# Opening three quarters of the first tile's layer_in one pair of heads at a time

## The chip, the cores and the metric

The kernel runs on one NeuronCore of a Trainium2 chip. The time is the device time of one execution in microseconds (us), median of three. The core has five engines that follow their own instruction lists: PE (matmul and transpose), DVE (vector), ACT (activation), POOL, and SP, which issues the loads and stores.

## What is computed

A sparse attention, a first feed-forward layer with the activation h * cos(h), and a layer of eight experts of which each token uses one:

```
scores = (q @ k.T) / 8                      # 2 batches x 8 heads x 576 x 576
scores = where(scores >= 32nd largest of the row, scores, -1e9)
x = softmax(scores) @ v                     # -> 1152 tokens x 512
h = x @ w_in                                # 512 -> 2048
x = (h * cos(h)) @ w_out                    # 2048 -> 512
expert, gate = argmax, max of softmax(x @ w_gate)
out = gate * (relu(x @ w1[expert]) @ w2[expert])
```

The weights w_in and w_out arrive as 64-bit numbers; the kernel converts them to 32-bit ones itself.

## The kernel before

**Attention** runs in 36 steps. A step takes 128 queries of a pair of heads (a few steps are shaped otherwise). `scores` makes a 128 x 576 score matrix for each head of the pair in one PSUM tile S (two banks, one tile only), half at a time; a copy on ACT or DVE puts the first half into Sp. `pair_chain` folds the halves on DVE into C and finds the 32 largest of each row by MAX8 and MATCH_REPLACE8 (lines 852 to 859). `softmax` subtracts the penalty, takes exp on ACT (L900) and scales. `products` transposes the result in three groups of three (tile pt, two banks, L927), copies each to PT, and multiplies by v into av (L941, L943). An ACT copy (L980) stores av as one quarter, one pair of heads, of the tile's input xn.

**Tiles.** Four steps make up one tile of 128 tokens; tile 0 takes steps 0 to 3. `layer_in` (L1021 for the first two tiles) computes its 2048 hidden features in four units u of four blocks of 128: for each block it adds four matmuls, kc = 0 to 3, one for each quarter of xn, in one PSUM bank, h. So no matmul of unit u of tile 0 could start before step 3 had filled the last quarter. The unit is copied to hs and its bank is free for the next one; there is one h bank. Then follow a clamp, the cosine, the product, and `layer_out` (L1106), which adds 16 blocks in one of the two banks x2. A routing step, a scatter and a gather lead to the experts (L1472 to L1536).

**Weights.** `convert(n)` turns block n of the weights into 32 bits: a load, an ACT operation whose result `lo` is held in a PSUM bank (L698), a conversion wt on ACT or POOL, and one or two DVE operations of which one reads `lo` (L704, L712). For n below 16 it is w_in, n = 4u + kc. The bank of `lo` is taken from the two banks x2.

**Unread products.** `unread` (L1264) makes 24 groups of eight bf16 matmuls of a constant by itself in the early part. They are written to a bank of x2 and never read.

**The order.** Each operation has a number. ORDER lists all of them; a program goes through the list, gives each operation its buffers and appends it to its engine's instruction list, so an engine's order is fixed when the kernel is built, and an engine waits where the next instruction of its list waits. PICKS says for each operation that could run on two or three engines which one has it. A tile that shares a `tag` with another shares its buffers.

Of the kernel before, what the change touches and what calls it, by code (L numbers as in the profile page):

```python
# [8 lines left out]
F32 = mybir.dt.float32  # L9
F32R = mybir.dt.float32r  # L10
BF = mybir.dt.bfloat16
I32 = mybir.dt.int32
# [37 lines left out]
    "0000020000000000000000210000000020000000020001000200010000110000000200000000000010000010000000010000"  # L50
    "0000000000000210101000000100000000000001000000000000000010000000000000000001100001000000010000000010"
    "0000000100022000000000000010002101000010000000001000000020000110010000000000100100010000000002111011"
    "0221110101220010111020010110111011111000110011101111111100000000100000000100111100100101011101110101"
    "0111011100001111110100111111110101000000000000000001110110110110010000100000010001000011011011010001"
    "0100000100000101011101110110000100010101001001111010000000000000000000100001110100010111010101011101"
    "011010101001")
ORDER = [
# [192 lines left out]
GROUPS = (0, 1, 2, 4, 6, 8, 9)  # L250
PLAIN = 2
UNCUT = 6
UNREAD = 24


class Nothing:
# [293 lines left out]
def forward(ctx, lasting, tc, kq, vn, vs_, w_in, w_out, w_gate, w1, w2, out, paired):  # L550
# [448 lines left out]
    def transposes(kp, src):  # L999
        for c in range(4):  # L1000
            PE.transpose(T[kp][:, c * 128:(c + 1) * 128], src()[:, c * 128:(c + 1) * 128], ident)

    def layer_in(t, u):


# [662 lines left out]
```

## Time and profile before

| | us |
|---|---|
| runs (three) | 632.49, 634.88, 634.97 |
| median | 634.88 |
| profiled execution | 633.3 |
| its span, first to last instruction | 631.5 |

The span is cut into stretches below. "Busy" is the time in which an engine has an instruction running. PE's matmuls overlap in the records, so the time from one start to the next is the better cost of one. The column PEclk is the granted clock of PE as a share of 2.4 GHz; where no change of it is on record it reads 1.00, and then the matmuls' own durations tell the level.

### The profile page before, as it was taken

To read this page: it belongs to the slowest core of one execution; us is meant where nothing else is said; L and a number is where in the kernel's file an instruction comes from. 1 tells how busy PE (TensorE), PEld (TensorE's weight loads), DVE (VectorE), ACT (ScalarE), POOL (GpSimd) and SP (SyncE) were. 2 spreads that over 40 slices of the span, in tenths; PEclk is the share of its full clock that TensorE was granted. 3 is DMA by queue.
4 is the path that set the end of the run, shared out by engine and by line. 5 is a ranking of instruction groups with operands and counts; after the bars stand their busy time and mean duration, and the time that the engine had idled before them with its cause. 6 is when DMAs were issued, how large, how long until landed. Compare 5 with 4: busy or idle time off the path is not lost.

```text
span 631.5 us, 11976 instructions
## 1 busy us (share of the span) xinstructions
PE 581.7 (92%) x4000; PEld 457.4 (72%) x4000; DVE 523.9 (83%) x1503; ACT 482.5 (76%) x999; POOL 338.9 (54%) x441
## 2 busy tenths in 40 slices
PE   2486999999999999999999999999889999999994
PEld 0264685675568767777677887888679898888993
DVE  5999999999999999999999896475466788878772
ACT  4899899999988888989788767546536686876762
POOL 3678778898886887856667343135661021020111
PEclk9998799999999999999999999999979999999998
DMA  8857995522343322331212100343356778776740
GB/s 318 302 158 247 330 376 184 183 61 69 108 122 88 87 83 68 109 109 46 88 45 83 43 22 19 109 142 117 122 168 201 221 253 246 220 237 224 230 146 17
DMA packets 44614, 94.64 MB, mean 150 GB/s; under 512 B 7165, under 2 KB 11261, under 8 KB 44544
## 3 DMA queue, kind: packets, MB, share of 16 engines
q1 hardware_dynamic: 42800, 89.04, 44.4%
q0 software_dynamic: 1744, 4.76, 2.0%
q8 instruction: 33, 0.54, 0.4%
q14 instruction: 37, 0.30, 0.1%
HBM read 81.87 MB, written 12.69 MB: 150 GB/s over the span
## 4 chain that ended last, share of the span: by engine, by line
PE 50%; DVE 12%; ACT 7%; issue 6%; POOL 2%; POOLq 0%; DVEq 0%; ACTq 0%
PE yp L1517 8%; PE x L1106 6%; PE x L1114 5%; PE hp L1472 5%; PE av L941 3%; PE hp L1477 3%; PE h L1031 3%; PE pt L927 2%; PE h L1033 2%; PE h L1032 2%; PE S L812 2%; DVE C L855 2%; PE h L1026 2%; DVE W L852 2%; PE hp L1475 1%
## 5 line engine op out<-in xcount | busy, mean ns | idle before, releaser
L897 POOL TENSOR_TENSOR Sp<-Sp,pen 128x576 f32<-128x576 f32 x67 | 86.6, 1292 | 31.3 <-ACT pen L893 31.1
L855 DVE MATCH_REPLACE8 C<-W,C 128x288 f32<-128x288 f32 x216 | 94.8, 442 | 0.0
L852 DVE MAX8 W<-C 128x8 f32<-128x288 f32 x216 | 93.2, 450 | 1.5
L1522 POOL DMA_INDIRECT out_dram<-ot,ti x16 | 17.2, 1073 | 127.5 <-DVE ot L1536 92.7
L812 PE MATMUL S<-kq 64*128 64x288 f32 x256 | 52.9, 493 | 27.0 <-DVE C L840 11.7
L1106 PE MATMUL x<-wo,hs 128*128 128x512 f32 x148 | 75.2, 607 | 0.1
L893 ACT ACTIVATE pen<-Sp,tb 128x576 bf16<-128x576 f32 x72 | 55.6, 772 | 6.4 <-POOL Sp L897 3.7
L927 PEld LDWEIGHTS pt<-ident,Sp 128*128 128x128 f32 x324 | 38.1, 143 | 28.1 <-issue 10.1
L900 ACT ACTIVATE Sp<-Sp,tb 128x576 f32<-128x576 f32 x72 | 55.7, 774 | 3.3 <-POOL Sp L897 1.7
L927 PE MATMUL pt<-ident,Sp 128*128 128x128 f32 x324 | 52.5, 282 | 4.5 <-ACT lo L698 2.1
L812 PEld LDWEIGHTS S<-kq 64*128 64x128 f32 x256 | 21.1, 200 | 47.1 <-issue 22.9
L1033 PE MATMUL h<-xh,wl 128*128 128x256 f32 x192 | 54.1, 282 | 0.0
L859 DVE MAX8 W<-C 128x8 f32<-128x576 f32 x72 | 52.9, 752 | 0.8
L670 ACT ACTIVATE PT<-pt 128x384 f32<-128x384 f32 x92 | 43.3, 486 | 10.4 <-PE pt L927 9.7
L840 DVE TENSOR_TENSOR C<-S,Sp 128x576 f32<-128x576 f32 x64 | 47.4, 749 | 3.3 <-ACT Sp L670 2.1
L670 ACT ACTIVATE Sp<-S 128x576 f32<-128x576 f32 x59 | 38.1, 646 | 9.9 <-PE S L812 7.2
L941 PEld LDWEIGHTS av<-PT,v 128*64 128x64 f32 x320 | 35.9, 142 | 13.1 <-issue 4.0
L941 PE MATMUL av<-PT,v 128*64 128x128 f32 x320 | 44.4, 287 | 0.9 <-DVE xl L974 0.8
L943 PE MATMUL av<-PT,v 128*64 128x128 f32 x320 | 44.2, 287 | 0.3 <-ACT PT L670 0.2
L1477 PE MATMUL hp<-xgs,la 128*128 128x192 f32 (+2 forms) x160 | 39.7, 251 | 0.0
L1472 PE MATMUL hp<-xgs,wk 128*128 128x384 f32 x128 | 38.9, 361 | 0.1
L1090 POOL TENSOR_TENSOR hs<-hs,ur 128x512 f32<-128x512 f32 x25 | 32.8, 1316 | 11.2 <-ACT ur L1081 11.1
(225 smaller groups left out, 1883.1 us busy)
## 6 DMA issues: line engine op xcount, KB each, us to landing
raw<-in_w_dram SPq DMA_DIRECT2D x64, 512.0 KB, 3.9
kq<-in_kq_dram SPq DMA_DIRECT2D x40, 288.0 KB, 2.9
v<-in_vn_dram SPq DMA_DIRECT2D x32, 320.0 KB, 3.5
wraw<-in_w_in_dram SPq DMA_DIRECT2D x16, 512.0 KB, 5.3
wraw<-in_w_out_dram SPq DMA_DIRECT2D x16, 512.0 KB, 4.2
xs<-z SPq DMA_DIRECT2D x1, 4680.0 KB, 19.0
v<-in_vs_dram SPq DMA_DIRECT2D x8, 320.0 KB, 3.3
out_dram<-z SPq DMA_DIRECT2D x1, 2304.0 KB, 24.2
```

The costliest lines, as they stand in the source:

```text
L670: P.flex([("act", act, lambda: ACT.activation(*args(), AF.Copy, scale=scale), False), ("dve", dve, lambda: DVE.tensor_scalar(*args(), scal ...
L812: PE.matmul(T[kp][:, a, 0:HS], t[p, S:S + 128], t[p, i * HS:(i + 1) * HS], start=True, stop=True)
L852: P.op("dve", 0.372, lambda r=r, i=i: DVE.max(T["W", s][:, i, LIST[r]:LIST[r] + 8], T["C", s][:, i, 0:HS]), r=[("C", s, i)], w=[("W", s, i)])
L855: P.op("dve", 0.42, lambda r=r, i=i: DVE.match_replace(T["C", s][:, i, 0:HS], T["W", s][:, i, LIST[r]:LIST[r] + 8], T["C", s][:, i, 0:HS], ...
L897: eng.tensor_tensor(out=T["Sp", s][:, i, :], in0=T["Sp", s][:, i, :], in1=T[kp], op=OP.subtract)
L900: P.op("act", 0.76, lambda i=i: ACT.activation(T["Sp", s][:, i, :], T["Sp", s][:, i, :], AF.Exp, bias=T["tb", s][:, i, 1:2], scale=0.125, ...
L927: PE.transpose(T[kp][:, c * 128:(c + 1) * 128], P2[:, cc * 128:(cc + 1) * 128], ident)
L941: PE.matmul(o[0:64, 0:128], v[:, c * 64:(c + 1) * 64], chunk(c), start=(c == 0), stop=(c == 4), skip_group_check=True)
L1033: PE.matmul(o, lo, a, start=False, stop=(kc == 3), skip_group_check=True)
L1106: P.op("pe", 0.87, lambda f=f, a=a: PE.matmul(T["x2", t], T[kh][:, a:a + 128], T["wo", f], start=(f == 0), stop=(f == 15)), r=[kh, ("wo", ...
L1472: PE.matmul(o, hi_at(ka)[:, c:c + 128], x.rearrange("p a n -> p (a n)"), start=(kc == 0), stop=False, skip_group_check=True)
L1477: PE.matmul(T[kp][:, 0:n], T[kb][:, c:c + 128], x[:, 0, sl], start=False, stop=(kc == 3), skip_group_check=True)
```

## The change

Three things in the code, and a new order:

1. For tile 0, units 0, 1 and 2, `layer_in` no longer issues matmuls. `part_in(t, u, kc)` issues, for one quarter kc, the four matmuls of a unit into a bank that stays open from kc = 0 to kc = 3. Unit 0 has the h bank, units 1 and 2 have the two banks of x2 under the new name `ha`. The same 48 matmuls are issued; unit 3 is done as before.
2. `lo` takes its bank from the two banks of pt, the transposes' own, and no longer from x2.
3. `UNREAD = 0`: the 24 groups of unread products are gone.
4. ORDER and PICKS are new throughout. Read against the numbering of the operations, the lists say: up to the first scores of step 9 the order differs most. PE's list for steps 0 to 3 now reads `av 0, part_in (2,0), part_in (0,0), scores 4 (first half), part_in (1,0), scores 4 (second half), pt 1 ... av 1, scores 5, part_in (0,1) ...`, numbers in brackets being u and kc; the three sets of kc = 3 come right behind av 3 and scores 7. w_in is converted in the order n = 0, 4, 1, 5, 8, 10, 9, 2, 11, 7, 6, 3, 12, 13, 14 and 15, against 1, 2, 5, 6, 4, 8, 0, 7, 11, 9, 10, 3, 12, 13, 15 and 14. From the scores of step 9 on PE's list holds the same operations in nearly the same places. The load of w_gate goes from place 18 to place 61 of SP's list.

```
-UNREAD = 24
+UNREAD = 0
+EARLY = 3
...
-    ring("pt", "ps", [128, 512], F32, 2)
+    ring("pt", "ps", [128, 512], F32, 2, tag="pt")
...
-    ring("lo", "ps", [128, 512], I32, 2, tag="x2")
+    ring("ha", "ps", [128, 512], F32, 2, tag="x2")
+    ring("lo", "ps", [128, 512], I32, 2, tag="pt")
...
+    def by_steps(t, u):
+        return paired and t == groups[0][0] and t in plain and u < EARLY
+
+    def part_in(t, u, kc):
+        kp, w = part_of(t, u), (u, kc)
+
+        def mm():
+            for c in range(4):
+                PE.matmul(T[kp][:, c * 128:c * 128 + 128], T["ws", w][:, c * 128:c * 128 + 128], T["xn", t][:, kc],
+                          start=(kc == 0 and c == 0), stop=(kc == 3), skip_group_check=True)
+        P.op("pe", 0.9, mm, r=[("xn", t, s) for s in steps_of[t] if steps[s][3] == kc] + [("ws", w)], w=[kp])
+
+    def part_of(t, u):
+        return ("ha" if by_steps(t, u) and u else "h", (t, u))
...
     def layer_in(t, u):
-        kp, kh, ku, kn = ("h", (t, u)), ("hs", (t, u)), ("ur", (t, u // 2), u % 2), ("nn", (t, u))
+        kp, kh, ku, kn = part_of(t, u), ("hs", (t, u)), ("ur", (t, u // 2), u % 2), ("nn", (t, u))
...
-        for c in range(n):
+        for c in range(0 if by_steps(t, u) else n):
...
+        for kc in range(4):
+            for u in units:
+                if by_steps(t, u):
+                    part_in(t, u, kc)
```

## Rows read from the trace of the kernel before

**Rows 1.** The page: engines over the whole span, then tenths busy in 40 slices.

```profile
PE 581.7 (92%) x4000; PEld 457.4 (72%) x4000; DVE 523.9 (83%) x1503; ACT 482.5 (76%) x999; POOL 338.9 (54%) x441
...
PE   2486999999999999999999999999889999999994
...
DVE  5999999999999999999999896475466788878772
ACT  4899899999988888989788767546536686876762
```

**Rows 2.** Windows: stretch, its length, busy time (count) by engine, granted clock, DMA.

```profile
0.00:28.00 28.00, 7.84 (x24) 3.12 (x24) 19.70 (x48) 16.50 (x29) 14.04 (x34) 1.00 0.86 304
...
28.00:64.40 36.40, 26.78 (x287) 20.95 (x285) 35.26 (x94) 34.01 (x67) 29.08 (x38) 0.94 0.67 216
64.40:79.00 14.60, 14.38 (x103) 10.67 (x104) 14.03 (x43) 12.53 (x26) 11.71 (x14) 0.79 1.00 343
79.00:158.00 79.00, 76.36 (x559) 53.02 (x557) 76.14 (x212) 78.14 (x151) 66.84 (x86) 1.00 0.51 174
158.00:379.00 221.00, 217.64 (x1567) 162.20 (x1566) 208.07 (x615) 186.13 (x355) 155.24 (x203) 1.00 0.28 79
398.00:451.00 53.00, 52.91 (x344) 43.55 (x344) 30.29 (x83) 27.34 (x51) 23.00 (x29) 1.00 0.40 129
474.00:591.00 117.00, 116.76 (x699) 105.62 (x698) 91.81 (x259) 84.47 (x219) 15.32 (x14) 1.00 0.71 227
```

**Rows 3.** PE's timeline: start, duration, operation, idle time before it and its releaser.

```profile
28.07 5.83 PE L1264 MATMUL idle<-tri 128*128 128x128 bf16 x48
...
64.39 1.33 PE L812 MATMUL S<-kq 64*128 64x288 f32 x4 [4.87 <-issue]
...
82.64 0.49 PE L927 MATMUL pt<-ident,Sp 128*128 128x128 f32 x3
...
83.12 0.76 PE L812 MATMUL S<-kq 64*128 64x288 f32 x4
83.93 3.84 PE L1021 MATMUL h<-xn,ws 128*128 128x128 f32 x32
87.69 0.76 PE L812 MATMUL S<-kq 64*128 64x288 f32 x4
```

**Rows 4.** Groups by shape: operation and count, busy time, mean ns, idle before.

```profile
L1264 PE MATMUL idle<-tri 128*128 128x128 bf16 x192 | 16.2, 236 | 2.1 <-DVE wt L712 1.6
```

**Rows 5.** The same view of DVE from 16 to 170 us alone.

```profile
L671 DVE TENSOR_SCALAR PT<-pt 128x384 f32<-128x384 f32 x5 | 2.7, 549 | 0.2
...
L911 DVE TENSOR_SCALAR Sp<-Sp,sm 128x576 f32<-128x576 f32 x5 | 2.8, 555 | 0.0
...
L661 DVE TENSOR_TENSOR wl<-ws,wh 128x512 fp32r<-128x512 f32 x2 | 1.7, 868 | 0.0
...
L671 DVE TENSOR_SCALAR Sp<-S 128x576 f32<-128x576 f32 x2 | 1.5, 752 | 0.9 <-PE S L812 0.9
```

**Rows 6.** ACT's and DVE's timelines: first `lo`, a held `lo`, xn, step 15's last MAX8s.

```profile
4.80 0.63 ACT L698 ACTIVATE lo<-wraw 128x512 int32<-128x512 uint32 x1 [2.77 <-DMA wraw<-in_w_in_dram]
...
45.16 0.64 ACT L698 ACTIVATE lo<-wraw 128x512 int32<-128x512 uint32 x1
...
46.99 0.25 ACT L980 ACTIVATE xn<-av 128x128 f32<-128x128 f32 x1
...
48.89 0.68 DVE L712 SCALAR_TENSOR_TENSOR wt<-wt,lo 128x512 int32<-128x512 int32 x1
...
168.07 1.41 DVE L859 MAX8 W<-C 128x8 f32<-128x576 f32 x2
```

**Rows 7.** The chain of work that ended last, in order of time: start, duration, what.

```profile
137.61 0.67 ACT pen L893
...
152.22 0.76 ACT PT L670 x2
...
157.14 1.06 PE x L1106 x2
```

More of the change, by code (lines that the diff above doesn't have):

```diff
@@ L49 @@
 PICKS = (
[L50 to L56, printed above, removed]
-ORDER = [
[187 rows of a table removed]
+    "0000000000000020000000200000000020000000020000000220000000020000000220000000200110000000010000020100"
+    "0000000000001001100000001100000000000000000000000000000110000000000000000000200001000000000000000010"
+    "0001000010002000000022000000000101000002100000002100010020000010000110010000100000021000001120000001"
+    "0220100001110000011020110101101110111101011001111110000000000000000000001000010111111111010101111111"
+    "1111111100001011111111110111010101010000000000000000110110110010010101010000000000011001011011010100"
+    "0010000100000001000100101100100100110111011001110000000000000000000000000000000110010010010101010000"
+    "010101111111")
+ORDER = [
[186 rows of a table added]
 ]
```

373 rows, old and new, of the table ORDER are left out of this document.

## Prediction

> **What bounds the kernel now.** The page comes first [rows 1]: PE is busy for 92% of the span, DVE for 83%, ACT for 76%. The slices say that this is an average over stages: PE is full from the fifth slice or so to the last but one, DVE is full until the middle and then falls, ACT is full early and then falls. So the windows come next, cut where the slices change [rows 2]. Each row is a stage, and what is to be read is length minus busy time, the idle time of an engine in it:
>
> Up to 28 us PE works 7.8 us and DVE 19.7. From 28 to 64.4 PE shows 26.8 us of 36.4, but 16.2 of these are the unread products [rows 4], all of which start in this stretch; real work is 10.6 us. So PE has 25.8 us that are empty or filled with products nobody reads. DVE is idle for 1.1 us there and ACT for 2.4. From 64.4 to 158 PE is idle for 2.9 us, DVE for 3.4 and ACT for 2.9: three engines are full at once, and no view alone says which of them sets the pace. The chain of waits runs along ACT from 137 to 153 and then passes to PE [rows 7]. From 158 to 379 PE is idle for 3.4 of 221 us, DVE for 12.9 and ACT for 34.9: PE bounds here. It also does after attention, with 0.1 us idle from 398 to 451 and 0.2 from 474 to 591. So a microsecond taken off PE's work behind 64.4 us is worth one at the end if PE can use it, and PE's early hole is where work can go.
>
> **What is moved on PE.** 32 matmul instructions of `layer_in` (16 matmuls, two instructions each) take 83.93 to 87.69 with nothing between them, 3.76 us [rows 3]. Three units are 96 instructions, 11.3 us at full clock. In before all of them lie behind 64.4. In the new list nine of the twelve sets (kc = 0 to 2), 8.5 us, come ahead of `av 3` and so can fall into the hole; the three of kc = 3 stay where PE is full. They fit: 10.6 + 8.5 = 19.1 us of 36.4.
>
> Also the stretch 64.4 to 71 may gain. PE had been idle for 4.87 us before the score matmuls at 64.39, and these took 1.33 us where those at 83.12 took 0.76 [rows 3]; the granted clock of 64.4 to 79 is 0.79 [rows 2]. Read as a part at 1.2 GHz and the rest at 2.4, that is 2 x 0.21 x 14.6 = 6.1 us at the lower level, and 3.1 us lost. With parts to do PE would not stand idle there. PE's own bound is thus 8.5 to 11.6 us.
>
> **What is removed.** 192 unread instructions, 16.2 us [rows 4], all in the hole. The direct gain is nothing, since PE waits there anyway; what hides it is that DVE, not PE, is 97% busy from 28 to 64.4. The indirect cost is the clock. The score matmuls ran at the slow duration wherever PE had been idle, and the first fast ones stand behind the 5.83 us of unread products that begin at 28.07 [rows 3]. Without these the early steps run at 1.2 GHz until the real work is dense. Bounds: nothing, if it is dense at once; at the other end everything in the hole at half speed, at most 2 x 19.1 = 38 us in 36.4, an overflow of 2 us. I take nothing: PE need not be early there.
>
> The Trainium skill says in "TensorE: Matmul & The Clock Gate", Part 1, that half rate is the default and sustained activity releases it, and under HAM oscillation that idle gaps bring it back. By that rule dropping the unread products gives the low clock to steps 0 to 3. The trace agrees as to the direction (1.33 against 0.76); by the rule the sum would come to no gain, as in the rival on the clock below.
>
> **What is added on the other engines.** The list of choices moves flexible operations. Up to step 15's last MAX8 DVE has lost its five scalings (0.555 each) and both score copies (0.752) [rows 5], 2.8 + 1.5 = 4.3 us. The rest (three PT copies of 0.549 and one subtraction more, two splits and a product fewer) cancels to within 0.3 us. DVE's list is thus 4.3 us shorter at step 15, but not evenly: the same length at step 3, 1.3 us shorter at step 7, 3.8 at step 9.
>
> ACT gets four weight conversions and two score copies (0.65 each) and loses four splits, three PT copies and an hs copy by step 15: the same within half a microsecond. On the way it has more, 3 us at step 7 and 5 at step 9. ACT's early idle time must pay for that: 11.5 us up to 28, of which 4.8 pass before the first weights land [rows 6], and 4.5 from 28 to 79 [rows 2]; about 11 us that can be filled. POOL is 85% busy at most, and its list is 1 us shorter at step 15.
>
> **Waits and queues.** A part waits for the xn copy on ACT, and behind it in PE's list stand the scores of step 4. The xn copy of step 0 ran at 46.99 [rows 6], late because 12 operations stood between the last PT copy and it on ACT; the new list has five, some 3 us. The scores that wait behind it are wanted by DVE only after chain 3, so the cost is nothing; without that cover it is up to 3 us, once. Weights (0,0), (1,0) and (2,0) are among the first five converted, well ahead. The h bank and both x2 banks are held from av 0 to the hs copies; nobody else asks for them, since `layer_out` of tile 0 comes later and `lo` has left. On SP the early loads keep their pace; w_gate is moved past 43 entries and is first used by routing, after tile 0's `layer_out`: nothing.
>
> `lo` now shares pt's two banks. A `lo` is held from its ACT operation to the DVE operation that reads it, 45.16 to 49.57 in one case [rows 6], 4.4 us, while 32 of them have to pass. Three transposes share a bank for about 1 us: 0.49 [rows 3] and a copy. A transposition that finds both banks held waits. Bounds: nothing, if the order always finds one free; 10 us, if half of the 18 groups of steps 3 to 8 wait for 1 us. Below nothing is not excluded, as `layer_out` no longer shares with `lo`. I take 0 to 1, as the lists interleave parts and transposes and PE has time until 64.4.
>
> **The sum.** At step 15 PE could be early by 8.5 to 11.6 us, DVE by 4.3 plus what it idles less, at most 3.4, and ACT by what it fills of its early 11 us less the 5 it has more on the way. The least of these decides: DVE, 4.3, about 4 with something for the shared banks. From there PE's list holds the same operations as far as step 35's `av` and beyond, and PE is full, so the lead is kept and does not grow; DVE's further saving lies beside it. Span 631.5 and profiled time 633.3 lose 4: 629.3. The median of the runs stands 1.6 above the profiled execution, so by it 630.9. I give **630.0**.
>
> **The rivals.** *DVE paces (forecast)*: 3 to 6 us off, 627 to 632. For it: DVE's 96 to 97% from 28 to 158.
> *PE alone paces*: then the whole 8.5 to 11.6 us comes through, 622 to 626. For it: PE's 97% from 64.4 and 99% later; against it: ACT and DVE are as full until 158.
> *ACT takes over*: its list is not shorter at step 15, and the chain runs on it from 137 to 153 [rows 7]. If it cannot fill its early idle time, nothing is left: 632 to 636.
> *The clock or bunched parts*: the low clock, or xn copies that come late, push the parts behind `av 3`; then PE does what it did, and the change does not do what it says: 632 to 635.
> *The shared banks (slower)*: from about 9 of the 18 waits of 1 us on, the 4 us are gone and PE, full behind 64.4, pays on; at all 18, and ACT's `lo` operations held with everything behind them, 4 to 8 us slower: 637 to 641.
>
> **Chances.** Forecast 0.46, PE alone 0.17, ACT 0.17, clock or bunching 0.10, banks 0.10. 80% needs the ends of the next cases: from 623 to 637. What can be told from no change is about 0.5%, 3.2 us. Faster by more: three quarters of the forecast and PE alone, 0.52; slower by more: the banks and a little of the rest, 0.12; same 0.36.
>
> **What would show it.** Right: parts of kc = 0 to 2 before some 65 us with PE less than full there; step 15's last MAX8s (168.07 before [rows 6]) some 4 us earlier; from there to the end a constant lead; DVE still 96% busy from 28 to 158 and PE with more idle time from 64 to 158 than 2.9 us. Wrong: a lead of 8 or more at step 15 (PE paced), none with ACT at 99% (ACT), score matmuls of 1.33 us far beyond 45 us (clock), or transposes that wait for DVE's reading of `lo` (banks). A lead at step 15 that is lost behind 398 would show that the tail does not follow attention.

## The result and the profile after

| us | before | after |
|---|---|---|
| median of six runs | 634.09 (632.49 to 634.97) | 626.50 (625.65 to 629.05) |
| profiled execution | 633.3 | 625.78 |
| its span | 631.5 | 623.9 |

After takes 0.9885 of the time of before, 95% interval 0.9863 to 0.9907: 7.3 us faster, 5.9 to 8.7. That is in the range of the prediction (623 to 637), 3.5 us below its value, and between two of its cases: DVE paces (627 to 632) and PE alone paces (622 to 626).

The page of after comes first, the engines over the span and three rows of the slices, to be read against [rows 1]:

```profile
PE 569.5 (91%) x3808; PEld 444.4 (71%) x3808; DVE 518.7 (83%) x1496; ACT 490.7 (79%) x1013; POOL 332.5 (53%) x434
...
PE   3277888999999999999999999999899999999994
...
DVE  5999999999999999999999984475666788878772
ACT  6799999999998889989787787556446788766861
```

PE has 192 instructions fewer, the unread ones, and is busy for 12.2 us less. In the fifth to the seventh slice its digits say 8 where they said 9: what it does early is now real work, with holes. ACT is fuller at the start. The windows of after show it by stage (length, then busy time and count of PE, PEld, DVE, ACT and POOL, granted clock, DMA), against [rows 2]:

```profile
0.00:28.00 28.00, 7.99 (x24) 3.11 (x24) 20.38 (x56) 19.36 (x34) 14.95 (x33) 1.00 0.86 309
28.00:64.40 36.40, 24.29 (x173) 17.26 (x173) 35.57 (x97) 34.66 (x70) 33.66 (x43) 1.00 0.77 252
64.40:79.00 14.60, 12.45 (x100) 9.79 (x102) 14.40 (x43) 14.60 (x31) 13.07 (x19) 1.00 1.06 387
79.00:158.00 79.00, 73.99 (x516) 47.22 (x516) 74.80 (x213) 78.25 (x149) 70.53 (x88) 1.00 0.46 156
158.00:379.00 221.00, 219.02 (x1582) 164.49 (x1578) 208.23 (x614) 191.70 (x358) 148.62 (x199) 1.00 0.25 76
```

From 28 to 64.4 PE does 24.3 us of real work, against 10.6. From 64.4 to 158 it is idle for 7.2 us, against 2.9: 4.3 us of the room that was made in its list stay empty there. ACT is now the full one there, 0.75 us idle in 93.6. Before 79 ACT is idle for 10.4 us, against 16.0. From 158 to 379 PE is idle for 2.0 us, against 3.4.

The parts and the scores around them on PE's timeline of after (start, duration, operation, idle time before and its releaser):

```profile
35.62 1.33 PE L813 MATMUL S<-kq 64*128 64x288 f32 x4
40.65 1.13 PE L1013 MATMUL ha<-xn,ws 128*128 128x128 f32 x8 [1.36 <-ACT xn L981]
41.62 1.06 PE L1013 MATMUL h<-xn,ws 128*128 128x128 f32 x8
42.61 0.76 PE L813 MATMUL S<-kq 64*128 64x288 f32 x4
43.29 1.16 PE L1013 MATMUL ha<-xn,ws 128*128 128x128 f32 x8
...
53.57 1.16 PE L1013 MATMUL h<-xn,ws 128*128 128x128 f32 x8 [1.82 <-ACT xn L981]
54.66 0.76 PE L813 MATMUL S<-kq 64*128 64x288 f32 x4
...
67.77 1.06 PE L1013 MATMUL ha<-xn,ws 128*128 128x128 f32 x8
...
72.94 1.95 PE L1013 MATMUL ha<-xn,ws 128*128 128x128 f32 x16
```

The nine sets of kc = 0 to 2 lie between 40.65 and 68.8, seven of them ahead of 64.4. The last slow score matmul (1.33) is the one at 35.62; once the first parts have run, the scores take 0.76 and stay so, while in before they fell back to 1.33 at 64.39 [rows 3]. So without any unread product PE holds its upper level from some 42 us on: the score matmuls from there to 79 us all take 0.76. It is the parts that stand there at that time; with nine of them put off (e2 below) scores take 1.33 again at 65.99.

The chain that ended last in after, some of its longest pieces (start, duration, what), against [rows 7]:

```profile
10.47 1.33 DVE C L841 x2
...
84.59 1.28 ACT L901
...
161.03 1.28 ACT L901
...
211.12 1.91 PE x L1123 x4
```

It is DVE's at the start, ACT's over most of steps 3 to 15 and PE's later. And step 15's last MAX8s on DVE, against [rows 6]:

```profile
161.74 1.41 DVE L860 MAX8 W<-C 128x8 f32<-128x576 f32 x2
```

They start at 161.74, against 168.07: 6.3 us earlier. The span ends 7.6 us earlier.

### The profile page after: what moved, and what is told of

It is laid out like the page before. It is cut to its first block, busy times and chain, and to the rows that moved or that the text cites. A ratio compares the mean times of both kernels' runs of the same rounds, so it can differ in the third digit from the quotient of the medians.

```text
span 623.9 us, 11585 instructions
## 1 busy us (share of the span) xinstructions
PE 569.5 (91%) x3808; PEld 444.4 (71%) x3808; DVE 518.7 (83%) x1496; ACT 490.7 (79%) x1013; POOL 332.5 (53%) x434
## 4 chain that ended last, share of the span: by engine, by line
PE 51%; ACT 24%; DVE 15%; issue 8%; DMA 1%; POOL 1%; SPq 0%; POOLq 0%; DVEq 0%; ACTq 0%
PE yp L1538 9%; PE x L1131 6%; PE hp L1493 5%; PE x L1123 5%; DVE C L856 4%; ACT Sp L901 4%; PE hp L1498 3%; DVE W L853 3%; ACT Sp L670 3%; ACT pen L894 3%; PE h L1048 3%; PE pt L928 3%; PE h L1050 3%; PE h L1049 3%; PE av L942 2%
## 5 line engine op out<-in xcount | busy, mean ns | idle before, releaser
L898 POOL TENSOR_TENSOR Sp<-Sp,pen 128x576 f32<-128x576 f32 x64 | 82.3, 1287 | 26.1 <-ACT pen L894 25.3
L1543 POOL DMA_INDIRECT out_dram<-ot,ti x16 | 16.6, 1036 | 127.7 <-ACT ot L1552 73.6
L1123 PE MATMUL x<-wo,hs 128*128 128x512 f32 x148 | 73.6, 603 | 0.0
L670 ACT ACTIVATE Sp<-S 128x576 f32<-128x576 f32 x66 | 42.6, 645 | 10.8 <-PE S L813 7.3
L670 ACT ACTIVATE PT<-pt 128x384 f32<-128x384 f32 x90 | 41.9, 485 | 8.3 <-PE pt L928 7.9
L942 PE MATMUL av<-PT,v 128*64 128x128 f32 x320 | 43.6, 283 | 2.3 <-ACT PT L670 1.4
L944 PE MATMUL av<-PT,v 128*64 128x128 f32 x320 | 42.8, 282 | 1.1 <-ACT PT L670 1.0
L1538 PE MATMUL yp<-wh,hc 128*128 128x512 f32 x96 | 37.5, 410 | 0.0
```

The costliest lines, as they stand in the source:

```text
L670: P.flex([("act", act, lambda: ACT.activation(*args(), AF.Copy, scale=scale), False), ("dve", dve, lambda: DVE.tensor_scalar(*args(), scal ...
L898: eng.tensor_tensor(out=T["Sp", s][:, i, :], in0=T["Sp", s][:, i, :], in1=T[kp], op=OP.subtract)
L942: PE.matmul(o[0:64, 0:128], v[:, c * 64:(c + 1) * 64], chunk(c), start=(c == 0), stop=(c == 4), skip_group_check=True)
L1123: P.op("pe", 0.87, lambda f=f, a=a: PE.matmul(T["x2", t], T[kh][:, a:a + 128], T["wo", f], start=(f == 0), stop=(f == 15)), r=[kh, ("wo", ...
L1538: PE.matmul(T[kp], x, w, start=(fc + n == 0), stop=(fc == 7 and n == len(uses) - 1))
```

## The experiments

**One table serves all of them.** It follows the same instruction through the kernels: the start of the last MAX8 over 576 columns in a step, read from the trace of DVE, as a difference to before (negative is earlier). e8 repeats these MAX8s in steps 4 to 11, which are left open. The second column is the ratio to before with its interval, from all executions; the steps are those of one profiled execution, which is the fastest of its kernel in e2 and e6 and the slowest in e8.

| kernel | ratio to before | step 0 | 3 | 6 | 7 | 9 | 12 | 15 | 25 | 33 | 34 |
|---|---|---|---|---|---|---|---|---|---|---|---|
| after | 0.9885 (0.9863, 0.9907) | -2.1 | -2.4 | -4.7 | -4.2 | -6.5 | -7.5 | -6.3 | -7.8 | -4.8 | -8.0 |
| e1 unread off | 0.9979 (0.9967, 0.9991) | -0.3 | -0.2 | -1.0 | -1.0 | -1.0 | -1.0 | -1.0 | -1.0 | -1.0 | -0.9 |
| e11 unread back | 0.9906 (0.9882, 0.9930) | -1.3 | -1.5 | -4.0 | -3.4 | -5.6 | -6.7 | -5.5 | -6.9 | -4.0 | -7.2 |
| e6 lo in pt | 1.0180 (1.0162, 1.0198) | -0.1 | 0.0 | 6.6 | 7.0 | 9.3 | 9.2 | 9.2 | 9.1 | 9.1 | 9.1 |
| e5 old order | 1.0262 (1.0224, 1.0300) | -0.3 | 0.0 | 13.7 | 14.2 | 17.1 | 16.9 | 16.8 | 16.8 | 16.8 | 16.9 |
| e12 one open | 1.0039 (1.0026, 1.0051) | 0.6 | 0.9 | 3.6 | 3.6 | 3.6 | 3.5 | 3.5 | 3.5 | 3.5 | 3.5 |
| e4 choices only | 1.0303 (1.0278, 1.0329) | 0.4 | 1.7 | 3.7 | 4.3 | 5.6 | 8.0 | 8.9 | 15.0 | 19.8 | 18.7 |
| e2 bunched | 1.0079 (1.0048, 1.0110) | -2.2 | -2.5 | -3.2 | 5.4 | 3.1 | 2.0 | 3.2 | 1.7 | 4.6 | 1.4 |
| e3 DVE back | 0.9943 (0.9926, 0.9960) | -2.1 | -2.3 | -3.8 | -3.4 | -5.6 | -5.6 | -3.7 | -5.5 | -2.5 | -5.8 |
| e7 ACT plus | 0.9985 (0.9973, 0.9998) | -1.9 | -2.2 | -4.5 | -2.5 | -2.4 | -2.0 | 0.6 | -0.9 | 2.1 | -1.1 |
| e8 DVE plus | 0.9955 (0.9939, 0.9971) | -2.1 | -2.4 | | | | -0.9 | 0.2 | -1.3 | 1.7 | -1.5 |
| e9 PE plus | 0.9952 (0.9933, 0.9970) | -2.1 | -2.4 | -4.8 | -3.0 | -4.9 | -5.6 | -3.0 | -4.5 | -1.5 | -4.7 |
| e10 PE plus, old | 1.0063 (1.0044, 1.0081) | 0.1 | 1.2 | 1.4 | 1.4 | 1.8 | 3.6 | 4.8 | 4.8 | 4.8 | 4.9 |

Between kernels with the same lists, where a row changes, time was won or lost; where it stays, nothing happened. DVE's list in after has another order than in before, so the row of after also changes with the place of a MAX8 in its list: from step 12 to 34 it swings between -4.8 and -8.2, with no clear trend. Rows of that order are best compared with the row of after.

Step 0 of the kernels with the lists of before differs by up to 0.9 us between executions (-0.3 to 0.6, e4 with its other choices left out), so a difference of that size that is there at step 0 is put down to no edit. e10, whose edit begins at step 4, is 1.2 us late at step 3. Differences between two kernels below are differences of their ratios times 634.1.

The granted clock differs too. From 64.4 to 79 us it is 1.00 in after, e3, e7, e8 and e11, 0.88 in e9, 0.84 in e1, 0.82 in e10, 0.79 in before, 0.77 in e2 and e12, 0.62 in e5, 0.54 in e4 and 0.50 in e6. The three slowest kernels have the lowest clock there. Whether it adds to their loss or only comes of PE's waiting in them, no run separates.

### The unread products

**e1_unread_off**, before without them:

```
-UNREAD = 24
+UNREAD = 0
...
+ORDER = [i if i < 9 else i - 24 for i in ORDER if not 9 <= i < 33]
```

> The kernel before with the 24 groups of unread products taken out and nothing else. Theory A (ACT and DVE set the pace up to step 15, PE's hole is only room): no change, within 1.5 us of before, since DVE is 97% busy while they run. Rival clock: score matmuls of steps 3 to 5 go back to 1.33 us and the steps behind them come late, 1 to 4 us slower than before. Rival in the other direction: the unread products held banks that lo waited for and PE waited with them, then 1 to 2 us faster.

Measured: 632.29 us, 1.3 us faster (0.6 to 2.1). Its stretch from 28 to 64.4 us, in the windows, and below it two lines of PE's timeline of before:

```profile
28.00:64.40 36.40, 18.73 (x94) 11.39 (x95) 35.82 (x95) 34.07 (x69) 29.44 (x38) 0.74 0.68 220
```

```profile
43.18 1.95 PE L1264 MATMUL idle<-tri 128*128 128x128 bf16 x24 [1.55 <-DVE wt L712]
45.06 0.76 PE L812 MATMUL S<-kq 64*128 64x288 f32 x4
```

The granted clock falls from 0.94 to 0.74, and yet the kernel is faster. So whatever the low level costs in these steps is less than what the products cost. That cost fits the rows of before: their bank is shared with `lo`, so a group waited 1.55 us for DVE's reading of a `lo`, and the scores of step 4 stood behind it. The lead, 0.2 at step 3, is 0.6 at step 4 and 1.0 from step 6 on. Only the growth at step 4 has this wait beside it; that at step 6 is not explained.

**e11_warm**, after with twelve groups of unread products put back, six behind the scores of step 2 and six between the operations from there to av 0:

```
-UNREAD = 0
+UNREAD = 12
+AT = {97: 6, 46: 1, 138: 1, 44: 1, 42: 1, 140: 2}     # number of the operation: groups put behind it
...
```

> The changed kernel with 12 of the groups of unread products put back, six behind the scores of step 2 and six between the operations up to av 0, so that steps 0 and 3 run at the full clock earlier. My term in the sum (the low clock there costs nothing): within 1 us of the changed kernel. Rival clock: 1 to 3 us faster than it.

Measured: 628.16 us, 1.3 us slower than after, with overlapping intervals. Some 0.9 of it are there at step 0 already, ahead of every group, and from then on the distance to after stays between 0.7 and 0.9. The scores take 0.76 from 33.70 on, against 42.61 in after, though the transposes at 48.60 are slow once more (0.90). Having PE at its upper level that much earlier gains nothing that can be seen.

### The shared banks

**e6_lo_in_pt**, before with the one edit of the banks:

```
-    ring("pt", "ps", [128, 512], F32, 2)
+    ring("pt", "ps", [128, 512], F32, 2, tag="pt")
...
-    ring("lo", "ps", [128, 512], I32, 2, tag="x2")
+    ring("lo", "ps", [128, 512], I32, 2, tag="pt")
```

> The kernel before with one thing changed: lo takes its bank from the two banks of the transposes and not from x2. This measures the shared banks by themselves, in an order not made for them. My term in the sum: 0 to 1 us slower than before. Rival (transposes that wait for DVE's reading of lo): 4 to 8 us slower, with PE's waits of pt for DVE's L712 in the trace.

Measured: 645.20 us, 11.4 us slower. By the table 9.2 us are made, all in steps 4 to 9. Waits from 28 to 110 us (engine, operation and line, whom it waited for: us in total, times, longest):

```profile
POOL sm L903 <- ACT Sp L900: 9.0, 5, 5.6
PE pt L927 <- ACT PT L670: 7.5, 7, 3.4
...
DVE C L840 <- ACT Sp L670: 4.9, 3, 3.3
...
ACT lo L698 <- DVE wt L712: 2.9, 3, 1.3
PE pt L927 <- DVE wt L712: 2.9, 3, 1.3
```

The direct waits for a shared bank are the last two lines, 2.9 us each in three. The rest is read as what follows from them: ACT is held at a `lo`, everything behind it on ACT comes later, and PE, POOL and DVE wait for ACT. Matmuls at the low level, the whole of 64.4 to 79 by the granted clock, may have a part in it. In after the same waiting, a transposition for DVE's reading of a `lo`, is 0.8 us, once from 28 to 158. So the rival of the shared banks is a real mechanism, and the edit costs more than the 10 us bound in an order not made for it; the new order avoids it.

### The parts

**e5_parts_old_order**: after's code, with the order and choices of before, and each part right behind the xn copy that it reads (of the edit, the lines of the order; `NEW` holds the new numbers of the operations).

```
...
+XN = {73: 0, 116: 1, 159: 2, 202: 3}       # number of the xn copy: kc
+ORDER = [n for i in ORDER for n in ([NEW[i]] if i in NEW else []) + [1839 + 3 * XN[i] + u for u in range(3) if i in XN]]
```

> The changed code (open banks, lo in pt's banks, no unread products) with the order and the choice of engines of the kernel before; the three parts of a quarter stand right behind the xn copy of that quarter. PE has its 8.5 us less behind 64.4 us, DVE and ACT have the lists of before. Theory A: DVE and ACT hold the steps back, 0 to 3 us faster than before. Theory P: 6 to 8 us faster, nearly the whole gain.

Measured: 651.35 us, 16.6 us slower. It holds the shared banks too, which alone are 11.4. Waits from 28 to 110:

```profile
ACT PT L675 <- PE pt L933: 13.7, 7, 5.0
...
DVE C L846 <- ACT Sp L675: 11.3, 3, 6.4
...
PE h L1018 <- ACT xn L986: 5.2, 4, 1.9
```

The parts wait for xn, the transposes stand behind them, ACT waits for the transposes, and DVE for ACT.

**e12_one_open** takes the banks out of it: before's order and choices, no unread products, `lo` in its old banks, and the parts of unit 0 alone, in the h bank that they use anyway.

```
-UNREAD = 24
+UNREAD = 0
+EARLY = 1
...
+ORDER = [n for i in ORDER for n in ([NEW[i]] if i in NEW else []) + [1839 + XN[i] for _ in range(1) if i in XN]]
```

> The kernel before, in its own order, without the unread products and with the parts of layer_in of the first quarter (unit) alone: they stand right behind the copies of xn that they read, in the bank that h uses anyway, so no bank is shared between two kinds of work. VectorE's and ScalarE's lists stay as before but for the products that go. About 2.7 us of TensorE's work stands earlier than before. Leaving out the unread products alone gave 0.9979, 1.3 us. Theory A (TensorE's moved work pays by itself): 1.3 + 2.7, about 4 us faster than before. Theory B (the step's chain on VectorE and ScalarE holds the steps, and TensorE's room is worth nothing without it): 1 to 2 us faster, as without the unread products alone. Rival (a part that waits for xn holds up the scores queued behind it): as before or slower, with the loss made in the steps in which the parts stand.

Measured: 636.08 us, 2.5 us slower than before and 3.8 slower than e1, from which only the parts differ (2.7 to 4.9 by the intervals). The rival holds for this run: work of PE, moved to where PE has empty time, cost more than it could have won. It was counted as 2.7 us, but its three sets took 2.08, 1.53 and 2.08, most of them at the low level. Of the 4.4 us between e12 and e1 at step 34, 0.9 are there at step 0, ahead of every part. The place of the largest loss, on the timelines of PE, ACT and DVE of e12:

```profile
70.14 0.90 PE L933 MATMUL pt<-ident,Sp 128*128 128x128 f32 x3 [1.48 <-ACT Sp L916]
70.88 2.08 PE L1018 MATMUL h<-xn,ws 128*128 128x128 f32 x8
72.74 0.85 PE L933 MATMUL pt<-ident,Sp 128*128 128x128 f32 x3
```

```profile
73.63 0.49 ACT L675 ACTIVATE PT<-pt 128x384 f32<-128x384 f32 x1 [1.67 <-PE pt L933]
...
75.27 0.65 ACT L675 ACTIVATE Sp<-S 128x576 f32<-128x576 f32 x1
```

```profile
75.95 0.76 DVE L846 TENSOR_TENSOR C<-S,Sp 128x576 f32<-128x576 f32 x1 [2.39 <-ACT Sp L675]
```

A part stands between two groups of transposes; ACT waits 1.67 us for the second, so its copy of the scores is late, and DVE, the full engine, stands for 2.39 us. In e1 DVE takes up the same operation without a wait. Here the clock may count: the eight instructions took 2.08 us at the low level, while in after they take 1.06 to 1.16. No run has these parts in the old order at the upper level.

**e2_bunched**, after with the nine sets of kc = 0 to 2 put back right ahead of those of kc = 3:

```
+PARTS = list(range(1839, 1851))
+at_ = min(ORDER.index(i) for i in PARTS[9:])
+ORDER = ([i for i in ORDER[:at_] if i not in PARTS] + PARTS[:9] + [i for i in ORDER[at_:]])
```

> The changed kernel with the nine parts of kc = 0 to 2 put off to right before those of kc = 3, behind av 3 and the scores of step 7; lists of the other engines as in the changed kernel. PE gets 8.5 us of work back behind some 70 us. Its idle time there in the changed kernel (2.2 us from 64.4 to 79 and 5.0 to 158) can take up part. Theory A: 1.5 to 4 us slower than the changed kernel. Theory P: 7 to 8 us slower, back to the kernel before. If PE has room enough: no change.

Measured: 637.40 us, 12.3 us slower than after, where 7 to 8 were the most that a theory gave. The first line below, of its DVE timeline, says why this doesn't measure PE's work alone; the other two are of PE's:

```profile
86.15 1.42 DVE L844 TENSOR_TENSOR C<-S,Sp 128x576 f32<-128x576 f32 x2 [7.81 <-ACT Sp L673]
```

```profile
65.99 1.33 PE L816 MATMUL S<-kq 64*128 64x288 f32 x4 [2.54 <-ACT Sp L673]
...
84.67 0.76 PE L816 MATMUL S<-kq 64*128 64x288 f32 x4
```

The twelve sets lie between the two halves of the scores of step 7, from 73.75 to 84.67, and DVE waits out most of them in one piece: 8.6 us between steps 6 and 7 of the table. (In after, too, the three sets of kc = 3 stand between these halves, not behind both.) That part shows what a long block ahead of scores costs, not what empty time on PE is worth.

But 1.5 us are lost by step 6 already (-3.2 against -4.7), ahead of the block, where PE has less to do than in after. Without the parts its granted clock is 0.77 from 28 to 79, the scores at 65.99 are slow again, and transpositions wait 2.1 us for DVE's reading of a `lo`, where PE's rows of after from 38 to 90 have no such wait. So the parts, where after has them, also keep PE at its upper level. Which of the two the 1.5 us belong to is not separated.

### The choices

**e4_picks_only**, before with the PICKS of after and its own ORDER.

> The kernel before, its order, but the changed kernel's choice of engines. DVE's list up to step 15 is 4.3 us shorter, ACT's as long, PE's work where it was. Theory A: DVE is freed but PE stays full from 64.4 us on with only 2.9 us of idle time up to 158, so 0 to 3 us faster than before. Theory P (the work moved on PE makes the whole lead): no change. If the choice of engines alone made the lead, 6 to 8 us faster.

Measured: 653.85 us, 19.2 us slower. The loss grows over all steps, 8.9 at step 15 and 18.7 at step 34. Choices are made for one order; this run doesn't price the five scalings and two score copies by themselves.

**e3_dve_back** does that, in after's order: the five scalings and two score copies are DVE's again.

```
+PICKS = "".join("1" if n in (23, 45, 58, 59, 86, 95, 118) else p for n, p in enumerate(PICKS))
```

> The changed kernel with the five scalings and two score copies of steps 2 to 13 put back on DVE; ACT loses five operations of 0.65 to 0.75 us, POOL two. DVE's list up to step 15 is 4.3 us longer, ACT's 3.5 us shorter. If DVE sets the pace: 4 us slower than the changed kernel. If ACT does (the chain of the changed kernel runs on it from 32 to 158 us): within 1 us or up to 2 faster. If PE does: no change.

Measured: 629.97 us, 3.7 us slower than after, 1.9 to 5.4 by the intervals. By the table it is 2.6 us at step 15 and 2.2 at step 34. DVE's list was counted to get 4.3 us longer. Up to step 15's last MAX8s DVE is busy for 5.2 us more than in after (154.0 against 148.8), since two of the five scalings took far more than the 0.50 to 0.74 us of the other three:

```profile
128.00 1.37 DVE L913 TENSOR_SCALAR Sp<-Sp,sm 128x576 f32<-128x576 f32 x1
...
137.58 1.51 DVE L913 TENSOR_SCALAR Sp<-Sp,sm 128x576 f32<-128x576 f32 x1
```

And it is idle for 2.5 us less (10.4 against 12.9). So half of the longer list goes into time that DVE waited in after, and only the other half arrives. Why the two scalings were slow wasn't tried.

### Which engine paces

Four kernels add some 5.4 us to one engine in steps 4 to 11 by doing an operation again; the results stay the same.

**e7_act_plus** (an ACT copy of Sp onto itself behind the second exp of a step), **e8_dve_plus** (the last MAX8 of a step twice), **e9_pe_plus** (two of three groups of transposes twice) on after, and **e10_pe_plus_old**, the transposes on before (the changed expressions alone):

```
+    ACT.activation(T["Sp", s][:, i, :], T["Sp", s][:, i, :], AF.Copy) for _ in range(i) if 4 <= s < 12      # e7
+    DVE.max(...) for _ in range(1 + i * (4 <= s < 12))                                                      # e8
-                for c in range(3):
+                for c in (*range(3), *range(3 * (g < 2 and 4 <= s < 12))):                                  # e9, e10
```

> The changed kernel with one ACT operation more in each of steps 4 to 11 (a copy of the second half of Sp onto itself behind exp), 8 x 0.67 = 5.4 us on ACT. If ACT sets the pace there: 4 to 6 us slower than the changed kernel. If DVE alone does: 0 to 1.5. If PE does: nothing.

> The changed kernel with the last MAX8 of steps 4 to 11 done twice, 8 x 0.68 = 5.4 us on DVE. If DVE sets the pace: 4 to 6 us slower than the changed kernel. If ACT alone does: 0 to 1.5. If PE does: nothing.

> The changed kernel with the first two groups of three transposes of steps 4 to 11 done twice, 16 x 0.33 = 5.3 us more on PE. Its PE idles for some 7 us between 64.4 and 158. Theory A (PE has room there in the changed kernel): 0 to 2 us slower than the changed kernel. Theory P: 5 us slower.

> The same 5.3 us of doubled transposes of steps 4 to 11 in the kernel before, whose PE idles for 2.9 us from 64.4 to 158. If PE sets the pace there in the kernel before: 4 to 6 us slower than before. If DVE and ACT do and PE only keeps up: 0 to 3. Beside e9 it says whether the change took PE off the path.

| engine with some 5.4 us more | slower than the kernel without | by the intervals |
|---|---|---|
| ACT, after | 6.3 | 4.7 to 7.9 |
| DVE, after | 4.4 | 2.7 to 6.2 |
| PE, after | 4.2 | 2.4 to 6.1 |
| PE, before | 4.0 | 2.8 to 5.1 |

If DVE alone paced, PE's time would have cost 0 to 2 us in after. It cost 4.2, as much as in before. The windows of e9 from 79 on:

```profile
79.00:158.00 79.00, 75.87 (x540) 51.17 (x541) 72.25 (x204) 76.33 (x144) 68.62 (x88) 1.00 0.46 153
158.00:379.00 221.00, 218.76 (x1576) 163.86 (x1575) 209.29 (x623) 191.85 (x361) 149.16 (x200) 1.00 0.26 77
```

PE is still idle for 3.1 us of 79, against 5.0 in after: most of the added time was not put into idle time, although there was some. A transposition lies inside a step's chain (scaled Sp on ACT, transposes on PE, the copy to PT on ACT, av), and time in it moves what follows, whether PE was idle elsewhere or not. The copy of e7 and the MAX8 of e8 lie inside that chain too. So the four runs show that no one of the three engines alone paces between steps 4 and 11, but they do not tell an engine's room from the length of the chain: no run adds time outside the chain.

ACT's time costs more than DVE's (the intervals of e7 and e8, measured together, do not overlap). In both the granted clock from 79 to 158 is 0.96, against 1.00 in after and e9, so a part of what they cost may be slower matmuls. In the table e10 goes from 1.2 at step 3, ahead of its edit, to 4.9, so 3.7 us are behind it.

## Why the prediction came out as it did

**The views and the hole: right.** PE had empty time early, the parts fit there, nine sets start ahead of 68 us, and the later stages are PE's. PE's idle time from 64.4 to 158 rose from 2.9 to 7.2, and DVE is still 96% busy from 28 to 158, as was said.

**The moved work, 8.5 to 11.6 us: not what came through.** It was PE's bound, and another list was taken to decide. In the list it went as worked out, and the clock of 64.4 to 79 is 1.00 instead of 0.79. But its worth by itself was never seen: in the old order the cleanest part of it (e12), at the low level, made the kernel slower by 3.8 us than without it.

**The unread products, 0 taken with bounds from 0 to a loss of 2: the sign was wrong.** They cost 1.3 us (e1), by the rows through a bank shared with `lo`, with scores queued behind a waiting group. The rows of before showed that wait; it was counted in the group's idle time [rows 4] and not followed to what stood behind it.

By "TensorE: Matmul & The Clock Gate" of the Trainium skill, Part 1, gaps in PE's work bring the half rate back. The trace agrees: 0.74 granted in e1. That this takes away the gain, as the rule was weighed in the prediction, isn't what e1 and e11 show. In e12 and e2, where slow matmuls lay in a step's chain, a loss stands beside it.

**DVE's list, 4.3 us at step 15: the size was right.** Less the 2.1 us of the start, the lead of after is 2.1 at step 7, 4.4 at step 9 and 4.2 at step 15, where 1.3, 3.8 and 4.3 were counted. Windows from step 3's last MAX8s to step 15's, before and then after, show the list itself:

```profile
49.91:168.07 118.16, 107.85 (x791) 74.97 (x789) 113.67 (x316) 114.74 (x222) 100.29 (x127) 0.96 0.59 197
```

```profile
47.52:161.74 114.22, 101.75 (x732) 67.70 (x733) 109.10 (x310) 112.64 (x220) 103.19 (x131) 1.00 0.58 198
```

DVE is busy for 4.6 us less and idle for 0.6 more, which makes the 3.9 that the lead grows by. That the list is shorter by what was counted is shown; that this makes the lead is not. PE is busy for 6.1 us less in the same stretch, and handing the seven operations back to DVE costs 2.6 us at step 15 and 3.7 at the end (e3), not the whole list. Part of the lead may also belong to the unread products.

**"The least of these decides": wrong as a picture.** The sum treated the three engines as lists of which the longest sets the end. The four runs with added time show that 5.4 us on any of them, inside a step's chain, cost 4 to 6. The chain of after runs on ACT through these steps, as the rival "ACT takes over" had it, but ACT did fill its early idle time (10.4 us left of 16.0), so its list did not become the later one. POOL was left out: its list was said to be 1 us shorter at step 15, but by those MAX8s it is busy for 135.9 us, against 131.2. No run adds time to POOL.

**The xn copies: right.** The first one of after runs at 40.26, against 46.99, and PE's parts wait 3.9 us for such copies in all. From 38 to 90 us DVE waits for no scores, so nothing of it arrives, as was said.

**The start, not counted at all: 2.1 us.** DVE's list was said to have the same length at step 3, and from this no lead. By count it has: the same twelve conversions of L712, three of L704 and of L707, 24 short and eight long MAX8s. But the end of step 3 comes 2.4 us earlier, 2.1 of them already at step 0. Windows from 0 to that end, before and then after (columns as above), and DVE's groups of L707 in the same stretch (count, busy, mean ns):

```profile
0.00:51.30 51.30, 28.97 (x270) 20.22 (x270) 42.69 (x110) 37.84 (x69) 32.29 (x55) 1.00 0.77 264
...
L707 DVE SCALAR_TENSOR_TENSOR ws<-wt,ws 128x512 int32<-128x512 int32 x3 | 2.6, 853 | 0.0
```

```profile
0.00:48.90 48.90, 21.42 (x104) 12.37 (x104) 41.10 (x110) 39.33 (x72) 34.12 (x56) 1.00 0.84 290
...
L707 DVE SCALAR_TENSOR_TENSOR ws<-wt,ws 128x512 int32<-128x512 int32 x3 | 2.0, 678 | 0.0
```

DVE's idle time is 7.8 us instead of 8.6, and its busy time for the same 110 instructions 41.1 instead of 42.7. Of the latter 1.6 us some 0.5 are one conversion of L707 that took 1.20 us in before, right behind the first fold; the rest is on no single line. Between the first fold and the last MAX8 of step 0 the new order also has three conversions where there were five, which is why the lead shows at step 0; the other two come later and don't take it back. So what is shown of the start is its size; its cause is read from the rows and not tested. e2, e3, e7 and e9, which have the order of after, have the same lead at step 0, as has e8, and e11 has 1.3 of it.

**The shared banks, 0 to 1 taken: right for this order,** 0.8 us waited. As a rival it was bounded too low: 11.4 us in the old order, where, by the waits, a held `lo` stops ACT's whole list.

**Kept to the end, no growth: as far as the rows tell.** The lead is 7.5 at step 12, 6.3 at step 15, 4.8 at step 33 and 8.0 at step 34, and the span shows 7.6. These swings come with the places of the MAX8s in DVE's two lists and are larger than any growth. PE's idle time from 158 to 379 fell by 1.4 us, which would allow as much. Why PE waits less there wasn't tried.

**The sum.** 2.4 up to step 3 and 3.9 from there to step 15 make 6.3 of the 7.6 us of the span; the other 1.3 have no place, by the swings. The prediction had 4, for the part behind step 3. So its term came out, and the number was missed by what it lacked, the start above all. That 626.5 stands in the range it owes to the other cases, since 627 to 632 was the forecast's own.

**What stays open.** The bank edit (11.4 slower), the choices (19.2 slower) and the parts (3.8 slower for one unit) each lose in the order of before; together in their own order they win 7.3. No run shows how the gain divides among them, nor what the new order would give without parts: e2 measured a long block instead. No run holds the clock of 64 to 79 us fixed either: it is lower in all three than in after. Behind step 34 the spans differ by up to 2.1 us more than the table: in e3, e7, e9 and e11 the granted clock from 440 to 480 us is 0.83, in before and after 0.87, and none of these edits touches that stretch.

## What to carry over

Empty time on an engine is not room if the work put there stands between links of the chain that feeds the full engine: look at what is queued behind it and who waits for that, and add a known time to each engine in turn, inside that chain and outside it, before calling one of them the pace. A choice of engines, a sharing of buffers and an order belong together: here the choice alone cost 19.2 us and the sharing alone 11.4, where all together gain 7.3. Follow one instruction per step through two traces: where both have the same lists it shows in which step time was won, which no share of busy time does; where the lists differ it swings with the instruction's place, here by 3.4 us.

## What had not been expected of the hardware

The eight matmul instructions of a part took 1.06 to 1.16 us at the upper level and 2.08 at the lower, but 36 us at a granted clock of 0.74 instead of 0.94 cost less than the unread products that had held it up, and the kernel was 1.3 us faster (e1). A granted clock of 1.00 in a row does not say that PE ran fast: in after's window from 28 to 64.4 it reads 1.00, while the scores at 35.62 took 1.33 us and those at 42.61 took 0.76. The same scaling on DVE took 0.50 to 0.74 us three times and 1.37 and 1.51 twice in e3, and one conversion 1.20 in before, where its like take 0.67; what made them slow was not tried.
